# A running sum kept by sixteen accumulating transfers from GpSimd's queue in place of fifteen additions, with the program's order written anew

## The chip, the core and the metric

The kernel runs on one core of a Trainium2 chip. The metric is the device time of one execution in microseconds (us), lower is better. The core's engines are TensorE (PE in the profile; PEld is its weight load), VectorE (DVE), ScalarE (ACT) and GpSimd (POOL); SyncE (SP) issues nearly all transfers. Each engine works through its own instructions in the order in which the program gives them, and an instruction that waits holds those behind it on its engine.

## What is computed

A transformer block over 2048 tokens of width 512: a linear attention with a learned feature map (32 heads of width 16), then a spatial-shift mixer with two gelu layers. The part that the change touches is the attention's denominator:

```python
phi_k = concat([softmax(pk), softmax(-pk)])      # 2048 tokens x 32 heads x 32
kv = einsum("bhsf,bhsd->bhfd", phi_k, v)
z  = einsum("bhsf->bhf", phi_k)                  # the sum of phi over the tokens
num = einsum("bhqf,bhfd->bhqd", phi_q, kv)
den = einsum("bhqf,bhf->bhq", phi_q, z)[..., None] + 1e-6
o = (num / den) @ wo
```

## The kernel before

The tokens lie in 16 tiles of 128 rows, two of them to a chunk of 256. The program has these stages, and one stage's end overlaps the next one's beginning:

- Up to about 23 us: the modulation vectors, the first weights, the first layer norm.
- About 23 to 150 us: for each chunk the layer norm, its transposes (`pt`) and split `hh`; then projections of the keys, values and queries. A key tile goes from PSUM (`pp`) through `softmax_in` (two reductions `k1` and a subtraction on VectorE into `ke`, the exponentials on ScalarE), a sum and a reciprocal `k2` on VectorE, and the product `ke <- ke, k2`, which is now phi of that tile, mostly on GpSimd. `kv_add` then lets PE add the tile's 32x64 products into `kva`, and adds the tile into `zacc` (`za` in the profile), 128 partitions x 1024 values, 512 KB. Query tiles go through the same softmax (`qt`, `q1`, `qe`) and are stored to `q_s` in device memory.
- At the end of that stage two products with a matrix of ones sum `za` over the partitions and spread it (`zbc`, one of the tiles called `const`).
- About 153 to 330 us, chunk by chunk (`phase_a`): the query tiles come back (`e`), `ez <- e, const` is their product with `zbc`, VectorE makes the denominators (`pz`, `q2`, `q3`, `q5`), `e <- e, q3` divides, VectorE turns the tile into `pT`, and PE multiplies `pT` with `kvb` (the numerators); then `oT`, the output projection, two layer norms (`n`, `h`), and the mixer's first layer (`nT`, `pa`). `split_w3` (`wr`, `ws`) prepares weights in between, and `load_w` makes the halves `w` of each weight (`w <- raw, w` is the subtraction that gives the low half).
- From about 325 us on: the channel mixer with its weights streamed from device memory (`wq`), its partial sums in `pa` and `ac`; PE alone sets the pace there.

All work is first recorded as operations of a `Plan`, numbered in the order of recording. The table `ORDER` then lists all 2800 of them in the order in which they are emitted; a letter behind a number (A, V, G) chooses another engine for it than the first (ScalarE, VectorE, GpSimd). The table `SLOT` says which buffer each tile takes, so two tiles in one buffer wait for each other. Both tables come from a planner outside the kernel, which uses the costs written in the calls of `plan.op` (the engine's time, and `land`, the time until a transfer has landed). Waits between engines are set from the tiles that an operation reads and writes.

Of the kernel before, what the change touches and what calls it, by code (L numbers as in the profile page):

```python
# [11 lines left out]
OP = mybir.AluOpType  # L12
# [153 lines left out]
)  # L166
SLOT = {
    "pp": "051437620517022653373705745013034226461611710656607547246172461505207616274027341060462123674114"
          "3625706350706774303670237",
    "bd": "ag",  # L170
    "w": "0423679a50486cd35b7089",
    "rk": "k53e1blf",
# [1207 lines left out]
```

## Time and profile before

| | |
|---|---|
| median of three runs | 572.0 us (570.32 to 572.49) |
| the profiled execution | 576.09 us, span from first to last instruction 574.2 us |
| mean granted TensorE clock | 0.991 |
| PE busy | 558.8 us (97% of the span) |
| DVE, ACT, POOL busy | 497.1, 337.7, 377.1 us |
| share of the 16 DMA engines | 64.1% of the span for the queue that SP issues to |

The profiled execution lies 4.1 us above the median, and 1.9 us of it lie outside its span. PE is the engine that sets the pace over nearly the whole span; what is left of it is spread over single places. Times of rows below are counted from the span's start; "idle before" is the time that an engine stood still ahead of a group.

### The profile page before, as it was taken

How to read it: one execution, taken by the hardware profiler on the slowest of the kernel's cores; microseconds unless marked ns; L12 is line 12 of the kernel's file. 1: busy time of each engine (PE TensorE's matmuls, PEld its weight loads, DVE VectorE, ACT ScalarE, POOL GpSimd, SP SyncE). 2: the span in 40 equal slices, each digit the busy share in tenths (PEclk: the TensorE clock that was granted, in tenths of full speed). 3: DMA queues.
4: the chain of work that ended last, by engine and by line, in shares of the span. 5: the costliest groups of instructions: out<-in, count | busy, mean ns of one | idle time of the engine just before them, and what ended most of it. 6: DMA issues, size and time to landing. Idle time of an engine off the chain costs nothing.

```text
span 574.2 us, 12213 instructions
## 1 busy us (share of the span) xinstructions
PE 558.8 (97%) x4460; PEld 505.6 (88%) x4460; DVE 497.1 (87%) x899; ACT 337.7 (59%) x802; POOL 377.1 (66%) x390
## 2 busy tenths in 40 slices
PE   9999999999999699999999999999999999999996
PEld 9988878878788478888779999988999999999996
DVE  3789999999989999999997779858789868987987
ACT  2889896623423678697678866675652443544440
POOL 2579899997689999999774746435442535322532
PEclk9799999999999999999999999998999999999999
DMA  9964640631487656767569999994797696647222
GB/s 330 316 209 148 194 155 20 220 90 56 142 293 248 206 171 192 274 209 230 185 222 330 297 303 324 327 312 131 282 297 275 237 319 230 184 139 302 74 74 74
DMA packets 56251, 123.79 MB, mean 216 GB/s; under 512 B 6304, under 2 KB 17824, under 8 KB 52096
## 3 DMA queue, kind: packets, MB, share of 16 engines
q1 hardware_dynamic: 55904, 122.95, 64.1%
q8 instruction: 35, 0.57, 0.4%
q14 instruction: 24, 0.20, 0.1%
q10 hardware_dynamic: 288, 0.07, 0.1%
HBM read 88.66 MB, written 34.34 MB: 214 GB/s over the span
## 4 chain that ended last, share of the span: by engine, by line
PE 54%; DVE 4%; DMA 4%; POOL 4%; issue 1%; ACT 1%; DVEq 0%; POOLq 0%; SPq 0%
PE pa L472 23%; PE ac L472 18%; PE pp L472 12%; DMA xb<-dram 2%; DMA dram<-yt 2%; POOL ez L421 1%; PE pt L481 1%; POOL e L421 1%; POOL ws L421 1%; DVE pp L438 1%; DVE tw L419 0%; POOL w L421 0%; DVE q L443 0%; DVE pz L443 0%; POOL rs L582 0%
## 5 line engine op out<-in xcount | busy, mean ns | idle before, releaser
L472 PE MATMUL pa<-bH,wq 128*128 128x256 f32 x840 | 108.1, 283 | 2.6 <-DVE cu L419 2.6
L472 PEld LDWEIGHTS pa<-bH,wq 128*128 128x128 f32 x840 | 104.0, 190 | 3.5 <-DVE cu L419 2.8
L472 PE MATMUL ac<-w,gg 128*128 128x256 f32 x840 | 106.6, 281 | 0.0
L472 PEld LDWEIGHTS ac<-w,gg 128*128 128x128 f32 x840 | 103.2, 188 | 0.9
L472 PE MATMUL pp<-w,hh 128*128 128x512 f32 x384 | 94.5, 398 | 0.0
L472 PEld LDWEIGHTS pp<-w,hh 128*128 128x128 f32 x384 | 70.5, 188 | 16.0 <-issue 0.5
L472 PE MATMUL pp<-w,sh 128*128 128x512 f32 x192 | 49.2, 399 | 0.0
L472 PEld LDWEIGHTS pa<-nT,w 128*128 128x128 f32 x384 | 46.4, 189 | 2.8 <-DVE nT L419 1.7
L472 PE MATMUL pp<-w,oT 128*128 128x512 f32 x192 | 47.4, 397 | 1.4 <-DVE oT L419 1.4
L472 PE MATMUL pa<-nT,w 128*128 128x256 f32 x384 | 47.6, 283 | 1.0 <-DVE nT L419 1.0
L472 PE MATMUL pp<-hh,w 128*128 128x256 f32 x384 | 48.0, 282 | 0.0
L472 PEld LDWEIGHTS pp<-hh,w 128*128 128x128 f32 x384 | 46.2, 188 | 2.0 <-issue 0.9
L421 POOL TENSOR_TENSOR gg<-cu,gg 128x256 fp32r<-128x256 f32 (+1 forms) x33 | 22.5, 692 | 33.9 <-PE ac L472 12.4
L472 PEld LDWEIGHTS pp<-w,oT 128*128 128x128 f32 x192 | 35.4, 188 | 9.9 <-DVE oT L419 2.0
L472 PEld LDWEIGHTS pp<-w,sh 128*128 128x128 f32 x192 | 34.7, 188 | 8.9 <-issue 1.6
L402 ACT ACTIVATE cu<-pa 128x512 f32<-128x512 f32 (+1 forms) x39 | 20.4, 529 | 37.5 <-PE pa L472 29.2
L421 POOL TENSOR_TENSOR ez<-e,const 128x1024 f32<-128x1024 f32 x14 | 34.3, 2456 | 4.9 <-ACT const L402 3.5
L582 POOL TENSOR_TENSOR rs<-mv,const 128x2 f32<-128x2 f32 x31 | 21.9, 707 | 18.2 <-ACT mv L589 16.1
L421 POOL TENSOR_TENSOR e<-e,q 128x1024 f32<-128x1024 f32 x15 | 30.2, 2026 | 2.1 <-DVE q L419 2.1
L402 ACT ACTIVATE qe<-qe 128x512 f32<-128x512 f32 x32 | 19.3, 626 | 20.6 <-POOL qe L421 17.5
L402 ACT ACTIVATE gg<-sg 128x512 fp32r<-128x512 f32 x35 | 21.6, 623 | 15.2 <-DVE sg L419 11.0
L421 POOL TENSOR_TENSOR ke<-ke,k 128x1024 f32<-128x1024 f32 x15 | 29.1, 1946 | 0.6 <-DVE k L446 0.6
(219 smaller groups left out, 1294.4 us busy)
## 6 DMA issues: line engine op xcount, KB each, us to landing
wq<-dram SPq DMA_DIRECT2D x32, 1024.0 KB, 6.8
dram<-ws SPq DMA_DIRECT2D x35, 256.0 KB, 3.1
xl<-in_x SPq DMA_DIRECT2D x32, 256.0 KB, 4.1
dram<-qe SPq DMA_DIRECT2D x16, 512.0 KB, 2.9
e<-dram SPq DMA_DIRECT2D x16, 512.0 KB, 4.2
raw<-in_w SPq DMA_DIRECT2D x18, 256.0 KB, 4.3
mod<-in_wmod SPq DMA_DIRECT2D x16, 256.0 KB, 4.3
dram<-xl SPq DMA_DIRECT2D x16, 256.0 KB, 3.4
```

Source lines behind the costliest of these rows:

```text
L402: nc.scalar.activation(o(), i(), func, **kw)
L421: pool = ("Pool", cost, lambda: nc.gpsimd.tensor_tensor(o(), a(), b(), op=op))
L438: nc.vector.scalar_tensor_tensor(o(), a(), get(s), b(), op0=op0, op1=op1, **kw)
L472: nc.tensor.matmul(o(), a(), b(), start=s, stop=e, **kw)
L481: nc.tensor.transpose(o(), i(), ident())
L582: plan.op("Pool", 540 + 10 * m, lambda: nc.gpsimd.tensor_tensor(r(), v(), mhalf[:, :m](), op=OP.pow), [r], [v, mhalf])
```

## The change

`kv_add` no longer adds. The first tile's phi is copied into `zacc` by a transfer issued from GpSimd's queue, and each of the other fifteen is added to it by a transfer that reads the tile, adds it to what stands in `zacc` and writes that back. That makes 16 transfers where there were 15 additions (the first addition took two tiles). Each of them reads and writes all of `zacc`, so it waits on GpSimd's queue until the one before has landed. The planner counted 1 us of GpSimd and 3 us until landing for each, and with other rates for transfers wrote both tables anew: nearly every line of `ORDER` and `SLOT` differs.

```diff
@@ ORDER, SLOT: all lines anew, the first of each
-    "0 3 247 12 45 6 249 38 156 2 52 58 26 55 11 1 248 39 13 46 14 8 47 48 40 49 41 158 157 61 7 42 5 43 44V 19G "
+    "13 3 157 6 45 2 5 159 158 38 26 55 52 58 8 0 34 61 321 4 30 21 89G 46 19G 20G 47 91 48 39 49 101 92G 50 11 9 "
-    "za": "7",
+    "za": "1",
@@ kv_add
         first.append(e)
         if tt_:
-            tt(zacc, first[0] if tt_ == 1 else zacc, e, OP.add, "any")
+            plan.op("Pool", 1000, lambda: nc.gpsimd.dma_start(zacc(), e(), accum_op=OP.add), [zacc], [zacc, e], land=3000)
+        else:
+            plan.op("Pool", 1000, lambda: nc.gpsimd.dma_start(zacc(), e()), [zacc], [e], land=3000)
```

What the new order looks like at three places (names carry the numbers of their buffers, which differ between the two programs).

First, GpSimd's queue in the middle of the key stage. Before, `za` additions stand among the products `ke <- ke, k2` and the parts of w3 (`ws`):

```order
L421 TENSOR_TENSOR za_190_846<-za_190_846,ke_224_1021 128x1024
L421 TENSOR_TENSOR ke_230_1056<-ke_230_1056,k2_251_1215 128x1024
L421 TENSOR_TENSOR za_190_846<-za_190_846,ke_230_1056 128x1024
L421 TENSOR_TENSOR ke_253_1219<-ke_253_1219,k2_275_1331 128x1024
L421 TENSOR_TENSOR ws_256_1225<-ws_256_1225 128x256
L421 TENSOR_TENSOR za_190_846<-za_190_846,ke_253_1219 128x1024
```

Now, counted from 0, these are transfers 3 (`ke_191`), 4 (`ke_213`) and 5 (`ke_198`), with what stands between them:

```order
L421 TENSOR_TENSOR ke_191_859<-ke_191_859,k2_228_1055 128x1024
L789 DMA za_210_947<-ke_191_859 128x1024
L421 TENSOR_TENSOR ws_242_1130<-ws_242_1130 128x256
L421 TENSOR_TENSOR ke_219_1017<-ke_219_1017,k2_251_1178 128x1024
L421 TENSOR_TENSOR ws_229_1061<-wr_120_510,ws_229_1061 128x256
L789 DMA za_210_947<-ke_213_953 128x1024
L421 TENSOR_TENSOR ke_198_880<-ke_198_880,k2_214_961 128x1024
L421 TENSOR_TENSOR ke_250_1176<-ke_250_1176,k2_261_1282 128x1024
L789 DMA za_210_947<-ke_198_880 128x1024
```

The tiles are no longer added in the order in which they become phi, and two or three other instructions stand between one transfer and the next.

Second, VectorE ahead of the reciprocal `k2_228`, on which transfer 3 rests (`pp_238` is the key projection of a later tile, `hh_247` a half of the chunk after it). In the new order it reads:

```order
L443 TENSOR_REDUCE k1_245_1148<-pp_238_1103 128x32
L411 TENSOR_SCALAR pt_230_1064<-pt_230_1064,const_65_259 128x256
L443 TENSOR_REDUCE k1_245_1148<-pp_238_1103 128x32
L446 RECIPROCAL k2_226_1036<-k2_226_1036 128x64
L419 TENSOR_TENSOR hh_247_1155<-pt_230_1064,hh_247_1155 128x512
L419 TENSOR_TENSOR ke_250_1176<-pp_238_1103,k1_245_1148 128x1024
L443 TENSOR_REDUCE k2_251_1178<-ke_219_1017 128x64
L446 RECIPROCAL k2_228_1055<-k2_228_1055 128x64
```

In the order before, the same stretch of VectorE's instructions holds two of the four additions that it did:

```order
L419 TENSOR_TENSOR za_190_846<-za_190_846,ke_183_810 128x1024
L419 TENSOR_TENSOR za_190_846<-za_190_846,ke_197_873 128x1024
L443 TENSOR_REDUCE k1_235_1118<-pp_233_1082 128x32 x2
L419 TENSOR_TENSOR hh_223_1016<-pt_206_908,hh_223_1016 128x512
L443 TENSOR_REDUCE k2_242_1147<-ke_224_1021 128x64
```

The additions are gone, and the reciprocal stands behind reductions of `pp_238` that have nothing to do with it.

Third, GpSimd from the last of the sum to the first product with `zbc`. Before:

```order
L421 TENSOR_TENSOR za_190_846<-za_190_846,ke_298_1505 128x1024
L421 TENSOR_TENSOR ke_319_1676<-ke_319_1676,k2_327_1768 128x1024
L421 TENSOR_TENSOR ke_311_1613<-ke_311_1613,k2_320_1678 128x1024
L421 TENSOR_TENSOR za_190_846<-za_190_846,ke_311_1613 128x1024
L421 TENSOR_TENSOR ws_237_1133<-ws_237_1133 128x256
L421 TENSOR_TENSOR ez_351_1954<-e_273_1324,const_347_1898 128x1024
```

Now transfers 13, 14 and 15, and behind them:

```order
L789 DMA za_210_947<-ke_298_1529 128x1024
L421 TENSOR_TENSOR ke_315_1677<-ke_315_1677,k2_325_1741 128x1024
L789 DMA za_210_947<-ke_315_1677 128x1024
L421 TENSOR_TENSOR ws_197_875<-ws_197_875 128x256
L789 DMA za_210_947<-ke_323_1712 128x1024
L411 TENSOR_SCALAR mod_240_1118<-mod_240_1118,const_45_186 128x512
L421 TENSOR_TENSOR w_346_1934<-raw_260_1279,w_322_1706 128x512
L421 TENSOR_TENSOR acc_293_1493<-acc_293_1493,mod_240_1118 128x512
L421 TENSOR_TENSOR ws_286_1439<-ws_286_1439 128x256
L421 TENSOR_TENSOR w_346_1934<-raw_331_1771,w_322_1706 128x512
L421 TENSOR_TENSOR ez_358_2026<-e_336_1815,const_354_1955 128x1024
```

Low halves of weights (`w <- raw, w`) that stood behind the first `ez` before stand ahead of it now. The products with ones stand a little later on PE: the matmuls ahead of them are the same but for 24 more of a query projection (`pp <- hh, w`, 128x256) and one more tile's 16 into `kva`.

More of the change, by code (lines that the diff above doesn't have):

```diff
@@ L40 @@
 ORDER = (
[125 rows of a table removed]
[125 rows of a table added]
 )
 SLOT = {
[L168 to L172, printed above, removed]
-    "xl": "3148067ekjf2b3k5lj53ea310b4kb36f9ej72ka7ja8ci0f3",
-    "st": "12701i7g069dej37c25di54f801d1e691",
-    "mv": "53bd32a2f80g169dej3ej87277g6ci84a",
-    "rs": "64eg45dji4af280g169fh9a5dbi3fhbde",
-    "nm": "89afch89j6bch5e137bcih54abfih84g2630cj40acehb9agj25370cf",
@@ L178 @@
-    "xn": "9h7d2i38lg461g7j",
-    "acc": "efj90c",
-    "mod2": "0213",
-    "kva": "3",
-    "za": "7",
-    "hh": "158bcd1e",
-    "pt": "34142601145004722001432070140451",
-    "raw": "c9j016dcegb32dj7fh6fich05376",
-    "k1": "2040342352052250",
-    "ke": "6480536481534086",
-    "k2": "3150104314340143",
-    "vv": "8ai2de3a2728lg8e",
-    "qe": "5792013575963459",
-    "q1": "1352115204253304",
-    "qt": "44b66g8g0c6k",
-    "mod": "5084351a2ihb3fhl",
-    "kvs": "6",
-    "pz": "5",
-    "q2": "03125452",
@@ L197 @@
-    "e": "9214026381032509",
-    "ez": "4548788095254818",
-    "q3": "1245043013013041",
-    "q5": "11215024",
-    "pT": "8681859658808758",
-    "oT": "bcece2e1",
-    "nT": "b1bcee11",
-    "n": "08j2j2ea6jhe5005",
-    "h": "g68l75c2a84legi9",
-    "gf": "25133058",
-    "sh": "271b2be0",
-    "pa": "230137237075120265423717201420003710223716262317332611112637",
-    "wr": "12776",
-    "ws": "546kld8ihlf8229d04k24h31g0aj1h33bg9",
-    "gb": "d",
-    "tw": "42241",
-    "bL": "19619160",
@@ L214 @@
-    "nb": "g19i1bbf641f9g1i",
-    "yt": "04jc2k8a4k84lkk3",
-    "bH": "37852370594053597856709424173812",
-    "tr": "1kjb59g9hehflf02",
-    "wq": "7a92ae1942e142a14e2142ea14aa241ae124",
-    "cu": "2lhb6acjfk05b4l29cfi56e3ab9jf08ecf7hi06g",
-    "gl": "e70k0k1i",
-    "ac": "73565436014546500146475061205431",
-    "gg": "82430784237689470624708634560438294352687102543987153894567039456827013298576140",
-    "sg": "g541542ehgjke1haj1i474g2lfc6g5a5415l69ek",
-    "xb": "8k387gh841b9j3c4",
-    "uu": "lf8c2aa1l9b6",
@@ L226 @@
-    "xc": "17e6b0517ialg825",
+    "pp": "310025647016523417562234574731201310560527164404207515162200742145522637756435042453503473755764"
+          "6456232662403100407456656",
+    "bd": "9a",
+    "w": "023467abe809d7c2aeb589",
+    "rk": "d586j1be",
+    "xl": "4103lik5146e0b4cgcl0b45djgk930i12bf8dc0l063f23f6",
+    "st": "410di20bg58gf16bdj5gh57d8922gf346",
+    "mv": "629f167fi4be258gf16f1be15b3ce2cj7",
+    "rs": "83bg39d1297ij40e238i6gf34a86a15bf",
+    "nm": "a57cehj548aec3hj60adhc397aihc40dj49aih097ec0jb7dih809gea",
@@ new lines @@
+    "xn": "kg2fcgi2981kd8eg",
+    "acc": "h33hld",
+    "mod2": "1023",
+    "kva": "3",
+    "za": "1",
+    "hh": "1589cd15",
+    "pt": "34027056465646277632207075053017",
+    "raw": "46cdjaf55ef193gf61ieah9ij8a2",
+    "k1": "0152312122504213",
+    "ke": "4503872450892765",
+    "k2": "4503450133255404",
+    "vv": "fgj5932b3bc1fi5e",
+    "qe": "7821333921596134",
+    "q1": "2304402153452213",
+    "qt": "920e81i8j958",
+    "mod": "j8hbf07d9d37cigj",
+    "kvs": "9",
+    "pz": "1",
+    "q2": "10451314",
@@ new lines @@
+    "e": "8047802905693258",
+    "ez": "3639217883206107",
+    "q3": "2352130240520532",
+    "q5": "00405143",
+    "pT": "3215738231100623",
+    "oT": "34575144",
+    "nT": "363775b1",
+    "n": "j1gj7fi91ibhf8kf",
+    "h": "23l80c75lj6g5b71",
+    "gf": "73591127",
+    "sh": "146514b8",
+    "pa": "472302073015637342706313405452116040257345626763442053310242",
+    "wr": "69674",
+    "ws": "8282d40fkc7796i7eh9e113df2hf02aefib",
+    "gb": "4",
+    "tw": "70813",
+    "bL": "94590138",
@@ new lines @@
+    "nb": "3g2k32ek2c961i9a",
+    "yt": "k637fchgh2j83ck3",
+    "bH": "65207869847158519793554369622730",
+    "tr": "cfeki370dh9ih2i2",
+    "wq": "365314630413604314630463106160413604",
+    "cu": "ld0e5bghk7d2ga7eicf39ghbdf0l36a1gh0ije3k",
+    "gl": "7jk1j538",
+    "ac": "26376173541052105367765316703524",
+    "gg": "02137261030426103476249583652347832769017985642107410371549685421785036297184503",
+    "sg": "ifklkic680h6859b83687i5c21987c7d68f6ad7g",
+    "xb": "1l0l52eak6lb9c1l",
+    "uu": "khfii72ab7jd",
@@ L227 @@
+    "xc": "9fjf0ag3j32256fk",
 }
```

248 rows, old and new, of the table ORDER are left out of this document.

## The prediction

> **What bounds the kernel now.** I read the page's busy line first, then who PE waited for, then busy time by stretch.
>
> ```profile
> PE 558.8 (97%) x4460; PEld 505.6 (88%) x4460; DVE 497.1 (87%) x899; ACT 337.7 (59%) x802; POOL 377.1 (66%) x390
> ```
> ```profile
> PE pp L472 <- DVE pT L758: 3.3, 3, 1.6
> PE pa L472 <- DVE cu L419: 2.6, 1, 2.6
> PE pp L472 <- DVE oT L419: 1.4, 1, 1.4
> PE pa L472 <- DVE nT L419: 1.0, 1, 1.0
> ...
> PE pp L472 <- DVE const L419: 0.5, 1, 0.5
> PE pt L481 <- ACT n L402: 0.5, 1, 0.5
> ```
> ```profile
> 80.00:100.00 20.00, 20.00 (x164) 16.40 (x164) 18.84 (x26) 13.39 (x30) 18.27 (x17) 1.00 0.12 38
> 100.00:125.00 25.00, 25.00 (x231) 20.26 (x230) 23.88 (x33) 12.68 (x24) 24.84 (x16) 1.00 0.54 167
> 125.00:150.00 25.00, 25.00 (x263) 21.52 (x263) 24.54 (x32) 9.46 (x17) 19.66 (x11) 1.00 0.21 66
> 150.00:175.00 25.00, 24.47 (x318) 20.89 (x317) 22.87 (x33) 8.54 (x19) 20.06 (x11) 1.00 0.78 262
> 175.00:200.00 25.00, 20.63 (x148) 16.54 (x146) 23.59 (x43) 13.39 (x33) 25.00 (x18) 1.00 0.64 210
> 200.00:225.00 25.00, 24.11 (x209) 20.09 (x210) 24.23 (x40) 20.44 (x47) 25.00 (x21) 1.00 0.56 179
> 550.00:574.00 24.00, 19.30 (x152) 18.57 (x151) 19.10 (x43) 3.99 (x12) 6.89 (x8) 1.00 0.20 67
> ```
>
> The waits are in us in total, times, longest; the stretches give stretch, length, busy PE, PEld, DVE, ACT, POOL, clock, DMA share, GB/s. PE is busy in all of 80 to 150 us, where the additions lie: faster engines there save nothing by themselves. What can be saved lies behind: 3.3 + 1.4 + 0.5 + 0.5 = 5.7 us between 170 and 205, while DVE and POOL are full; 1.0 (nT) and 2.6 (cu) later; some 4.7 at the end, where the last additions follow the last matmul. All PE work stays: the new order has the same 20 kinds of matmul in the same numbers. So the change can give some 9 us at most, and lose without limit if PE comes to wait.
>
> **What goes.** The additions:
>
> ```profile
> L421 POOL TENSOR_TENSOR za<-za,ke x10: 2390/2408/2436, 78.9 to 146.6; 128x1024 f32<-128x1024 f32 x10
> L419 DVE TENSOR_TENSOR za<-za,ke x4: 1210/1218/1656, 81.5 to 145.2; 128x1024 f32<-128x1024 f32 x4
> ...
> L472 PE MATMUL pp<-za,const x4: 591/592/592, 150.0 to 151.3; 128*128 128x512 f32 x4
> L421 POOL TENSOR_TENSOR za<-ke,ke x1: 2433/2433/2433, 64.6 to 64.6; 128x1024 f32<-128x1024 f32 x1
> ```
>
> 10 x 2.41 + 2.43 = 26.5 us of POOL and some 5.3 us of DVE are freed, all under a full PE: nothing by themselves.
>
> **Where PE now asks for the sum.** Before, at 149.97:
>
> ```profile
> 149.97 1.88 PE L472 MATMUL pp<-za,const 128*128 128x512 f32 x4
> 151.78 0.65 PE L472 MATMUL kva<-ke,vv 128*32 128x64 f32 x32
> 152.36 3.09 PE L472 MATMUL pp<-hh,w 128*128 128x256 f32 x24
> ```
>
> The matmuls ahead of it in the new order are one query projection (24, 3.0 us net) and one tile's kva (32 records, 0.6) more, so a PE that never waits asks at 149.97 + 3.6 = 153.5.
>
> **When the sum is there.** Each transfer waits for the landing of the one before. I call L the time from the end of one transfer's wait to its landing; no row shows one. First the place from which the chain runs tight. Transfer 3 needs the product of ke_191, and that the reciprocal k2_228, which VectorE has behind reductions of pp_238. Ahead of pp_238's end PE has 180 matmuls of 512 columns and 96 of 256, as many as ahead of the end of this row, with four transposes more and 16 kva fewer, which cancel:
>
> ```profile
> 84.50 3.05 PE L472 MATMUL pp<-w,hh 128*128 128x512 f32 x12
> ```
>
> That is 87.5. Durations of what follows:
>
> ```profile
> L443 DVE TENSOR_REDUCE k<-pp 128x32 f32<-128x512 f32 x32 | 20.5, 667 | 0.4 <-PE pp L472 0.3
> L419 DVE TENSOR_TENSOR ke<-pp,k 128x1024 f32<-128x1024 f32 x16 | 19.3, 1205 | 0.2
> L443 DVE TENSOR_REDUCE k<-ke 128x64 f32<-128x1024 f32 x16 | 19.2, 1200 | 1.2 <-ACT ke L402 0.6 <-issue 0.3
> L419 DVE TENSOR_TENSOR hh<-pt,hh 128x512 fp32r<-128x512 f32 x16 | 10.8, 679 | 0.3 <-ACT hh L402 0.2
> L446 DVE RECIPROCAL k<-k 128x64 f32<-128x64 f32 x16 | 8.6, 540 | 0.1
> L411 DVE TENSOR_SCALAR pt<-pt,const 128x256 f32<-128x256 f32 x12 | 6.4, 545 | 2.0 <-PE pt L481 1.9
> L421 POOL TENSOR_TENSOR ke<-ke,k 128x1024 f32<-128x1024 f32 x15 | 29.1, 1946 | 0.6 <-DVE k L446 0.6
> L421 POOL TENSOR_TENSOR w<-raw,w 128x512 fp32r<-128x512 f32 x13 | 17.1, 1312 | 4.0 <-ACT w L402 3.6 <-PE pp L472 0.3
> ```
>
> On VectorE 2 x 0.67 + 0.55 + 2 x 0.54 + 0.68 + 1.21 + 1.20 = 6.0, less some 0.2 since neighbours overlap: 93.3. Then POOL's product, 1.95: transfer 3 goes at 95.3. From there POOL has never more than about 4.2 us of other work between two transfers (ke_254's product and three parts of ws of 0.75 ahead of transfer 7), so for L from 4.4 up the landings alone set the pace: twelve links to transfer 15 and its own landing, 95.3 + 13 L. (Transfer 0 could go at about 73 by the same count, so transfers 0 to 2 bind only from L = 7.4.) PE waits X = 95.3 + 13 L - 153.5; the chain is in time up to L = 4.48, and each 0.1 us of L costs 1.3 us of PE. That is the term on which this forecast rests.
>
> **L from rows.** Transfers of known size (KB each, median us from issue to landing, then the one of 1 MB that starts between 250 and 300):
>
> ```profile
> dram<-qe SPq DMA_DIRECT2D x16, 512.0 KB, 2.9
> e<-dram SPq DMA_DIRECT2D x16, 512.0 KB, 4.2
> out_dram<-xb SPq DMA_DIRECT2D x4, 128.0 KB, 1.8
> wq<-dram SPq DMA_DIRECT2D x32, 1024.0 KB, 6.8
> ```
> ```profile
> wq<-dram SPq DMA_DIRECT2D x1, 1024.0 KB, 5.4
> ```
>
> Lower end: 2.9, as if the second read and the making of the transfer by GpSimd were free. Upper end: 6.8, as much data as is read here, on full DMA engines. Between: from 128 to 512 KB a store grows by 1.1 us, so 512 KB more by 1.5, which gives 4.4; the least crowded row of 1 MB says 5.4. GpSimd has still to make the transfer, for which I add the upper half of that gap: L = 5.0. It is nearest to the 1 MB row, since each transfer reads the tile and zacc, 2 x 512 KB, and the DMA engines are half busy or less there (0.54, 0.21). The Trainium skill, "DMA: Bandwidth & Descriptors", Anatomy of one DMA — SWDGE (gpsimd) path, puts a transfer from GpSimd at 2.0 us plus its bytes at 436 GB/s, an estimate of 3.2 us for 512 KB, by which the chain would be in time; no row before shows such a transfer. The Trainium skill, "Collectives: The Full Stack", The bandwidth ceiling, speaks against taking that figure: an add in the DMA engine reads two sources, and its rate was measured at about half a copy's; 2.0 + 2.4 = 4.4 would be that estimate, still just in time.
>
> **The sum.** With L = 5.0 the last landing is at 160.3 and X = 6.8 us. Behind it, POOL goes from the sum to the third chunk's numerators. Before:
>
> ```profile
> 153.16 5.32 POOL L421 TENSOR_TENSOR ez<-e,const 128x1024 f32<-128x1024 f32 x2 [3.46 <-ACT const L402]
> ```
> ```profile
> 204.75 0.67 PE L472 MATMUL pp<-pT,const 64*32 64x256 f32 x16 [0.56 <-DVE pT L758]
> ```
>
> Between the two POOL is nearly full. In the new order three subtractions w<-raw,w (1.31 each) and one smaller piece of w (0.9) of that stretch stand ahead of the first ez: 4.8 us less. The sum is asked for 3.6 later, so without X the numerators of that chunk come 1.2 us earlier, and of the 5.7 us that PE waits there some 4.5 stay. X adds in full: while PE stands at the products with ones, neither zbc nor ez can go on. The subtractions moved forward cost nothing; POOL does them while transfer 15 is under way (X also covers them). Other moves I take at nothing: from 215 to 569 us PE shows only 3.6 us of waits to win. The load of the transfers, 16 x 1 MB read and 0.5 MB written over some 85 us, falls where the DMA share is 0.12 to 0.54 and I cost it at nothing on SP's loads, which are issued well ahead.
>
> Behind the waiting transfers stand products that kva needs; the nearest is ke_198, behind transfer 4 (100.3 + 1 + 2 = 103.3), which PE wants at about 104; if it slips, PE waits there instead and the last wait shrinks by as much. Buffers of ke are held until landing; VectorE wants the one of transfer 8 (lands at 125.3) at about 135.
>
> Against the profiled execution: 576.09 + 6.8 - 1.2 = 581.7; against the median, 4.1 lower, 577.6 us.
>
> **Rivals.**
> 1. The chain is in time: L up to 4.5 (the interpolated stores, 4.4). X = 0: 572.0 - 1.2 = 570.8, no change that can be told (I take 0.5%, 2.9 us, as what a measurement of this kernel can tell). With L to 4.8 X is up to 4.1 and it still is none. Against it: it needs the transfer to be made by GpSimd at no cost.
> 2. Faster: in time, and the new order also takes away the waits for cu (2.6) and nT (1.0): 570.8 - 3.6 = 567.2. Its place is PE at 272 and 388; it decides if VectorE, with 5.3 us less behind it, has those two adds done before PE arrives. For it: both waits are on DVE. Against: the same number of other instructions was laid anew around them.
> 3. The transfer is much dearer, L = 5.8 to 6.8 (the crowded 1 MB row): X = 17 to 30, 588 to 601 us. For it: sixteen rows of DMA work in one queue with SP's; against: the load is light between 80 and 150.
> 4. The engine that makes the transfers holds the products: with over 2 us of POOL for each, POOL instead of landing paces the chain. It has the same end as L raised, 580 to 590, and is counted in 3 and in the forecast.
>
> **How the numbers follow.** The forecast (L 4.8 to 5.8, 575 to 588) has 0.45, rival 1 0.27, rival 2 0.16, rival 3 0.12. Slower: forecast and rival 3, less the share that other moves give back, 0.56; same 0.27; faster 0.17. The range leaves out most of rival 3 and the far end of rival 2: 567 to 589.
>
> **What would show it.** A row of POOL transfers za<-ke some 5 us apart from about 95 us on; the last landing near 160; PE idle some 7 us before pp<-za,const, with a transfer as releaser; POOL waiting between 95 and 160; waits of PE for pT of about 4 to 5 us as before. If the transfers land in 4.4 us or less, PE runs through at 153 and I am wrong; so also if reciprocals ahead of transfer 3 come earlier than counted.

## The result, and the profile after

| | before | changed |
|---|---|---|
| median of the runs side by side | 572.25 us (4 runs) | 592.29 us (4 runs) |
| ratio, 95% interval | 1 | 1.033 (1.029 to 1.037) |
| profiled execution, span | 576.09, 574.2 | 592.05, 590.3 |
| busy PE / DVE / POOL | 558.8 / 497.1 / 377.1 | 563.9 / 491.8 / 353.3 |

Slower by 20 us against a forecast of 5.6, and above the range of 567 to 589. The two profiled executions are only 16.1 us of span apart, because the one before had come out 4 us above its median; the accounts below go from one to the other.

Page of the changed kernel, busy line, and behind it whom TensorE waited for (us in total, times, longest):

```profile
PE 563.9 (96%) x4460; PEld 508.9 (86%) x4460; DVE 491.8 (83%) x904; ACT 339.2 (57%) x807; POOL 353.3 (60%) x381
```
```profile
PE pp L472 <- DMA za<-ke: 10.5, 1, 10.5
PE kva L472 <- DVE vv L411: 5.3, 1, 5.3
PE pp L472 <- DVE pT L758: 1.9, 1, 1.9
PE pp L472 <- DVE qe L419: 1.6, 1, 1.6
```

New waits: 10.5 + 5.3 + 1.6 = 17.4. Matmuls of the same number are 563.9 - 558.8 = 5.1 longer. Gone: all 2.6 for cu, 1.4 for oT, 0.5 + 0.5, and 1.4 of the 3.3 for pT; some 6.5 with smaller ones. 17.4 + 5.1 - 6.5 = 16.0 of the 16.1 us. Part of the 6.5 may belong to that one execution of the kernel before and not to the change: in the run of the old order with transfers (below) the wait for cu is 0.6 and not 2.6.

The timeline of TensorE (start, us, work, idle before it and what ended that) shows the two waits and the slow stretch behind each:

```profile
141.88 2.91 PE L472 MATMUL pp<-w,hh 128*128 128x512 f32 x12
150.08 1.94 PE L472 MATMUL kva<-ke,vv 128*32 128x64 f32 x64 [5.29 <-DVE vv L411]
151.94 4.32 PE L472 MATMUL pp<-w,hh 128*128 128x512 f32 x12
...
157.22 5.92 PE L472 MATMUL pp<-hh,w 128*128 128x256 f32 x48
173.68 3.78 PE L472 MATMUL pp<-za,const 128*128 128x512 f32 x4 [10.54 <-DMA za<-ke]
```

Twelve matmuls that take 2.91 us before the first wait take 4.32 behind it, and the four products with ones take 3.78 where they took 1.88. With the `kva` rows behind the two waits (1.94 and 1.66 for 64 that take 1.10 elsewhere) that is 2.25 us behind the first wait and 2.46 behind the second, 4.7 of the 5.1 us. (A third slow stretch, behind the 1.9 us wait for pT, has its like in the kernel before, behind the wait for cu.) TensorE asks for the sum at 157.22 + 5.92 = 163.1, not at 153.5, and gets it at 173.7.

GpSimd's timeline gives the transfers. Rows 4, 9, 10, 14, 15 and 16 of the sixteen:

```profile
94.86 0.90 POOL L789 DMA_DIRECT2D za<-ke  x1 [0.30 <-POOL ke L421]
...
123.01 0.88 POOL L789 DMA_DIRECT2D za<-ke  x1 [1.52 <-DMA za<-ke]
...
132.39 0.88 POOL L789 DMA_DIRECT2D za<-ke  x1 [5.27 <-DMA za<-ke]
133.00 4.13 POOL L421 TENSOR_TENSOR ke<-ke,k 128x1024 f32<-128x1024 f32 x2
...
153.67 0.87 POOL L789 DMA_DIRECT2D za<-ke  x1 [1.13 <-DMA za<-ke]
...
161.50 0.88 POOL L789 DMA_DIRECT2D za<-ke  x1 [4.98 <-DMA za<-ke]
...
169.11 0.89 POOL L789 DMA_DIRECT2D za<-ke  x1 [5.96 <-DMA za<-ke]
```

Transfer 3 goes at 94.86, as forecast (95.3). Transfer 15 goes at 169.11, twelve links later (a link is the time from the start of one transfer to the start of the next): 6.19 us each. By the times from issue to landing each of them starts 0.2 to 0.7 us behind the landing before it. The links are uneven: 9.38 from 123.01 to 132.39, 7.83 from 153.67, 7.61 from 161.50, and 4.9 to 6.0 for the other nine. The twelve take 14.25 us more than 12 x 5.0, and the three long ones make 9.8 of that. What three of them shared the DMA engines with stands in the views of the DMA work over these stretches (q0: GpSimd's transfers, q1: SyncE's loads and stores; packets, MB, share of 16 engines; then the transfer's time from issue to landing). First 132.39 to 137.5, where q1 carried nothing, then 153.67 to 161.5, then the longest, 123.01 to 132.39:

```profile
q0 software_dynamic: 144, 0.52, 54.2%
za<-ke POOLq DMA_DIRECT2D x1, 512.0 KB, 4.6
```
```profile
q1 hardware_dynamic: 509, 1.46, 55.5%
q0 software_dynamic: 144, 0.52, 39.2%
za<-ke POOLq DMA_DIRECT2D x1, 512.0 KB, 7.1
```
```profile
q1 hardware_dynamic: 816, 0.98, 37.6%
za<-ke POOLq DMA_DIRECT2D x1, 512.0 KB, 8.8
```

Alone a transfer lands 4.6 us behind its issue, beside 1.46 MB of other traffic 7.1, beside 0.98 MB 8.8. The third long link shared with 1.07 MB (7.0 us to landing), the other nine with 0.9 MB or less. The rate of that traffic does not put the links in order, though: the longest had less of it per us than four links of 5.5 to 6.0 us, in whose stretches the DMA share was 0.84 to 1.00, against 0.67 here. Why it took 9.38 us stays open.

The wait for `vv` comes from one of these links too. While GpSimd stands 5.27 us before transfer 9 (the row of 132.39), the products in its queue behind it stand as well (133.00). VectorE's timeline:

```profile
135.28 1.22 DVE L443 TENSOR_REDUCE k<-ke 128x64 f32<-128x1024 f32 x1 [5.44 <-POOL ke L421]
...
149.30 0.63 DVE L411 TENSOR_SCALAR vv<-pp 128x512 f32<-128x512 f32 x1
```

VectorE idles 5.44 us for such a product, and TensorE stands 5.29 us until `vv`, fourteen us further down VectorE's queue.

### The profile page after: what moved, and what is told of

Its sections match the earlier page's. It is cut to its first block, busy times and chain, and to the rows that moved or that the text cites. A ratio compares the mean times of both kernels' runs of the same rounds, so it can differ in the third digit from the quotient of the medians.

```text
span 590.3 us, 12230 instructions
## 1 busy us (share of the span) xinstructions
PE 563.9 (96%) x4460; PEld 508.9 (86%) x4460; DVE 491.8 (83%) x904; ACT 339.2 (57%) x807; POOL 353.3 (60%) x381
## 4 chain that ended last, share of the span: by engine, by line
PE 43%; DVE 7%; DMA 2%; issue 1%; ACT 0%; POOL 0%; SPq 0%; DVEq 0%; ACTq 0%
PE pa L472 20%; PE ac L472 18%; PE pp L472 4%; DMA dram<-h 1%; DVE pz L443 1%; DVE pp L438 1%; DMA xl<-dram 1%; DVE bH L419 0%; DVE xb L419 0%; DVE q L443 0%; DVE ez L419 0%; DVE nT L419 0%; DVE uu L419 0%; DVE oT L419 0%; DVE gg L419 0%
## 5 line engine op out<-in xcount | busy, mean ns | idle before, releaser
L472 PE MATMUL pa<-bH,wq 128*128 128x256 f32 x840 | 106.9, 281 | 0.0
L472 PEld LDWEIGHTS pp<-w,hh 128*128 128x128 f32 x384 | 71.8, 190 | 16.5 <-issue 0.2
L472 PE MATMUL pp<-hh,w 128*128 128x256 f32 x384 | 49.8, 288 | 1.6 <-DVE qe L419 1.6
L472 PEld LDWEIGHTS pp<-hh,w 128*128 128x128 f32 x384 | 48.1, 194 | 3.7 <-issue 2.8
L582 POOL TENSOR_TENSOR rs<-mv,const 128x2 f32<-128x2 f32 x31 | 24.5, 797 | 17.4 <-ACT mv L589 17.4
L789 POOL DMA_DIRECT2D za<-ke x15 | 13.2, 880 | 29.8 <-DMA za<-ke 23.7
L402 ACT ACTIVATE gg<-cu 128x256 fp32r<-128x256 f32 (+1 forms) x57 | 19.0, 356 | 19.9 <-PE ac L472 16.4
L419 DVE TENSOR_TENSOR cu<-pa,cu 128x512 f32<-128x512 f32 (+1 forms) x36 | 21.2, 597 | 10.3 <-PE pa L472 7.1
```

Of the source, the lines that this page charges most:

```text
L402: nc.scalar.activation(o(), i(), func, **kw)
L419: dve = ("DVE", 71 + 1.04 * o.n + 90 * (isps(a) and isps(b)), lambda: nc.vector.tensor_tensor(o(), a(), b(), op=op))
L472: nc.tensor.matmul(o(), a(), b(), start=s, stop=e, **kw)
L582: plan.op("Pool", 540 + 10 * m, lambda: nc.gpsimd.tensor_tensor(r(), v(), mhalf[:, :m](), op=OP.pow), [r], [v, mhalf])
L789: plan.op("Pool", 1000, lambda: nc.gpsimd.dma_start(zacc(), e(), accum_op=OP.add), [zacc], [zacc, e], land=3000)
```

## The experiments

Two theories. **T**: the transfers lose the time, since GpSimd's queue waits for each landing. **R**: the new order starves TensorE whoever adds.

**Additions in the new order** (each fourth on VectorE; the first tile is copied by an instruction of GpSimd):

```diff
-plan.op("Pool", 1000, lambda: nc.gpsimd.dma_start(zacc(), e(), accum_op=OP.add), ...)
+eng = nc.vector if tt_ % 4 == 3 else nc.gpsimd
+plan.op("Pool", 2332, lambda: eng.tensor_tensor(zacc(), zacc(), e(), op=OP.add), ...)
```

> The new order and buffers, with the sixteen transfers turned back into one copy and fifteen additions at the same places (three of four on GpSimd, each fourth on VectorE). Theory T (the loss comes from the transfers: their landings hold up GpSimd's queue, and what stands behind it starves the matmuls): the waits for vv (5.3 us), qe (1.6) and for the sum (10.5) and the 5.1 us of slower matmuls go, the 6.5 us of waits recovered later stay: 565 to 574 us. Rival R (the new order itself starves the matmuls, whoever adds): 585 us or more, with a wait of 4 us or more between 140 and 175 us.

579.11 us against 572.76 of the kernel before, run beside it; ratio 1.010 (1.008 to 1.013). Between the two forecasts: the wait for the sum is gone, but the one for `vv` stands:

```profile
PE kva L472 <- DVE vv L411: 4.1, 1, 4.1
```

By this run 13 of the 20 us go with the transfers, and I had to ask whether VectorE's four additions (one took 2.95 us at 137.87) or the order made the rest.

**All additions on GpSimd:** as above with `eng = nc.gpsimd` throughout.

> The new order with the copy and all fifteen additions on GpSimd (15 x 2.4 us), none on VectorE. If the 4.1 us wait for vv in the new order with additions came from the four additions that VectorE had there, it goes, and GpSimd's last addition comes 3 to 8 us after the products with ones are asked for: 573 to 580 us. If it is the order itself, the wait for vv stays at 4 us: 578 to 584 us.

582.37 us against 574.64; ratio 1.013 (1.009 to 1.017). The two forecasts overlap and the kernel before ran 2 us slower beside it, so the total does not decide between them; the wait for `vv` does, which stays, at 5.6 us, so it was not made by VectorE's four additions. The stretches (length; busy PE, PEld, DVE, ACT, POOL; clock, DMA share, GB/s) suggest why:

```profile
100.00:125.00 25.00, 23.66 (x192) 20.03 (x191) 17.77 (x24) 13.29 (x27) 24.84 (x17) 1.00 0.41 138
125.00:150.00 25.00, 22.72 (x169) 18.51 (x167) 24.30 (x30) 7.64 (x15) 24.84 (x15) 1.00 0.25 82
```

GpSimd is busy 24.84 of 25 us twice over; in the kernel before it was 24.84 and 19.66. The new order has filled the room that the additions left there, and with them back TensorE waits for GpSimd's products (2.3 us) as well as for `vv`. So far R holds: with additions in it this order starves TensorE.

**Transfers in the old order** (the first addition stays):

```diff
-            tt(zacc, first[0] if tt_ == 1 else zacc, e, OP.add, "any")
+            if tt_ == 1:
+                tt(zacc, first[0], e, OP.add, "any")
+            else:
+                plan.op("Pool", 1000, lambda: nc.gpsimd.dma_start(zacc(), e(), accum_op=OP.add), ...)
```

> The order and buffers of the kernel before, with its first addition kept and the other fourteen turned into accumulating transfers at the same places of the order, all on GpSimd's queue. T: the chain of landings is late at the products with ones here too, and the products behind it in GpSimd's queue are late: 580 to 600 us. R: the transfers cost little by themselves: 570 to 576 us.

601.68 us against 572.76; ratio 1.050 (1.046 to 1.053), as T has it and a little above its range:

```profile
PE pp L472 <- DMA za<-ke: 20.4, 1, 20.4
```

The chain loses in both orders. The old order's own loads are enough to lengthen it: the last eleven transfers, from 106.84 on, take 4.5 to 8.4 us from issue to landing, 5.7 on average, where the changed kernel's thirteen from transfer 3 on take 5.6. The two slowest (7.1 and 8.4) lie beside 1.2 and 1.6 MB of other traffic, the four fastest (4.5 to 4.7) beside 0.5 MB or less.

**Two accumulators**, tiles in turn, everything else as in the changed kernel:

```diff
-    zacc = T("za", [P, 2 * D])
+    zacc = [T("za", [P, 2 * D]), T("const", [P, 2 * D])]
...
+        za = zacc[tt_ % 2]
...
-        mms([(..., ones, zacc[:, j * D:(j + 1) * D], True, True)], ...)
+        mms([(..., ones, zacc[i][:, j * D:(j + 1) * D], i == 0, i == 1) for i in range(2)], ...)
```

> The changed kernel with two accumulators that take the transfers in turn, so that each transfer waits for the landing of the one but last; the products with ones add both up (four more records of 0.59 us, 2.4 us of TensorE). T: no wait of GpSimd for a landing over 2 us, no wait of TensorE over 2 us near 145 and 165: 566 to 576 us. R: as the changed kernel plus 2.4 us: 590 to 596 us. If a transfer's landing is as late as it is because the DMA engines are full rather than because the chain waits, two in flight land later each, and some 4 to 8 us of the waits stay: 577 to 585 us.

The first tile of each accumulator is copied, so there are two copies and fourteen accumulating transfers. Some small constants share a buffer to make room for the second accumulator.

577.10 us against 572.76; ratio 1.007 (1.004 to 1.010), and 15 us under the changed kernel though TensorE has 2.4 us more to do. The profile shows no wait of GpSimd for the landing of a transfer any more, and of TensorE's new waits there are left:

```profile
PE pp L472 <- DMA const<-ke: 2.5, 1, 2.5
PE pp L472 <- DMA za<-ke: 1.0, 1, 1.0
```

That settles T against R for the bulk: the order is the same, and but for the one more copy so are the transfers; each now waits for the landing of the one but last instead of the last. It does not come out quite as T had it: 577.10 lies 1.1 above T's range and at the lower end of the third case, whose reason (4 to 8 us of waits left, since the DMA engines are full) is not far off: TensorE still waits 3.5 us for the last landings.

**Plain copies**; the sum is left out, the waits stay:

```diff
-nc.gpsimd.dma_start(zacc(), e(), accum_op=OP.add)
+nc.gpsimd.dma_start(zacc(), e())
```

> The changed kernel with plain copies in place of the accumulating transfers, each still waiting for the one before; the sum is left out (the last tile stays). If the second read of an accumulating transfer costs what its bytes do (Theory B), the link falls by some 1.2 us (half of the 2.4 us that the packets of the last transfer flow) and the wait for the sum is gone: 570 to 580 us. If the link is the making, the descriptors and the landing (Theory F), it stays at 4.5 us and more: 588 to 594 us.

576.78 us against 572.76; ratio 1.005 (1.002 to 1.008). The total is Theory B's, and so is the link: 61.0 us for the twelve from transfer 3 to 15, 5.09 each, 1.1 less than with the add (GpSimd waits 6.4 us for landings where it waited 23.7). But of the wait for the sum, which was to go, half is left.

```profile
PE pp L472 <- DMA za<-ke: 5.3, 1, 5.3
```

The wait for `vv` is gone. So what the add puts on top of a copy, over the length of the chain, makes most of the loss: 15.5 of the 20 us.

**The links by themselves:**

```diff
+    for i in range(6):
+        send(za, ke[i % 2])           # accumulate, alone
...
+    loads(30, 6)                      # SyncE: 512 KB each, six in flight
+    for i in range(6):
+        send(za, ke[i % 2])
...
```

> No layer is computed: stages of six 512 KB transfers from GpSimd's queue, each waiting for the landing before, (1) accumulating and alone, (2) plain copies and alone, (3) accumulating beside loads of 512 KB with six in flight, (4) beside loads with one in flight, (5) accumulating 256 KB and alone, (6) two chains in turn alone, (7) two chains beside six loads, (8) one chain beside back-to-back additions of VectorE. Theory C (the link is some 4.5 us by itself and grows with what else the DMA engines carry): start to start 4.5 to 5 us in (1), 3.3 in (2), 8 us or more in (3), 5 to 7 in (4), 3.2 to 3.8 in (5), 4.5 to 5 for a pair in (6). Rival S (the link grows with the work of GpSimd and VectorE, which share their way to memory): (3) and (4) as (1), and (8) 6 us or more.

GpSimd's timeline; the second and third transfer of the stages alone, copy, beside six loads, beside one load, 256 KB, two chains, beside VectorE:

```profile
23.55 0.87 POOL L371 DMA_DIRECT2D const<-const  x1 [3.98 <-DMA const<-const]
28.35 0.86 POOL L371 DMA_DIRECT2D const<-const  x1 [3.94 <-DMA const<-const]
...
53.51 0.54 POOL L373 DMA_DIRECT2D const<-const  x1 [2.61 <-DMA const<-const]
56.70 0.53 POOL L373 DMA_DIRECT2D const<-const  x1 [2.65 <-DMA const<-const]
...
82.70 0.87 POOL L371 DMA_DIRECT2D const<-const  x1 [9.75 <-DMA const<-const]
91.51 0.86 POOL L371 DMA_DIRECT2D const<-const  x1 [7.94 <-DMA const<-const]
...
134.94 0.86 POOL L371 DMA_DIRECT2D const<-const  x1 [4.75 <-DMA const<-const]
140.75 0.86 POOL L371 DMA_DIRECT2D const<-const  x1 [4.95 <-DMA const<-const]
...
180.19 0.88 POOL L371 DMA_DIRECT2D const<-const  x1 [2.77 <-DMA const<-const]
183.84 0.87 POOL L371 DMA_DIRECT2D const<-const  x1 [2.77 <-DMA const<-const]
...
211.59 0.86 POOL L371 DMA_DIRECT2D const<-const  x1 [2.00 <-DMA const<-const]
214.59 0.86 POOL L371 DMA_DIRECT2D const<-const  x1 [2.13 <-DMA const<-const]
...
317.06 0.88 POOL L371 DMA_DIRECT2D const<-const  x1 [4.04 <-DMA const<-const]
322.09 0.87 POOL L371 DMA_DIRECT2D const<-const  x1 [4.15 <-DMA const<-const]
```

Start to start: 4.80 alone, 3.19 for a copy, 8.81 beside six loads, 5.81 (5.6 to 6.8 over that stage) beside one, 3.65 for half the bytes, 3.00 with two chains (2.6 to 3.0 over that stage), 5.03 beside VectorE's additions. In the seventh stage, two chains beside six loads, a transfer takes 3.8 to 5.0, some 4.4 on average, half of one chain's 8.81. Theory C holds in every stage but the sixth, which I had put at 4.5 to 5 for a pair: two transfers in turn take 5.4 to 5.9 once both are under way. S is out: VectorE's work adds some 0.2 us at most. If the time is a straight line in the bytes, which two sizes cannot show, a link is some 2.5 us that do not go with the bytes (3.65 - 1.15) and 1.15 per 256 KB; the add takes 1.6 of the 4.80. And one load in flight on SyncE's queue gives links of the size that the changed kernel has on average (6.19).

**A wait and the clock:** bursts of 160 matmuls with growing waits between.

> No layer is computed: eight bursts of 160 matmuls (128x512, fp32r) on TensorE, and between them waits for GpSimd that grow from about 1 to about 13 us. Theory K (in the changed kernel TensorE's clock halves for some 4.6 us after its waits of 5.3 and 10.5 us, which makes the 5.1 us by which its matmuls are longer; waits of 1.6 us leave it alone): from some wait between 2 and 5 us on, the first some 4.5 us of the next burst are at 0.50, whatever the length of the wait, so that each long wait costs some 2.3 us more than itself. Rival: the slower stretch grows with the wait, or the clock falls for another reason and all bursts run alike.

Timeline, and the first 10 us of the second, third and eighth burst (length, busy PE, clock, DMA share, GB/s):

```profile
45.23 36.58 PE L345 MATMUL pz<-const,const 128*128 128x512 f32 x160 [0.92 <-POOL const L372]
84.06 38.16 PE L345 MATMUL pz<-const,const 128*128 128x512 f32 x160 [2.25 <-POOL const L372]
...
304.34 39.33 PE L345 MATMUL pz<-const,const 128*128 128x512 f32 x160 [10.65 <-POOL const L372]
```
```profile
45.23:55.23 10.00, 10.00 (x44) 1.00 0.01 2
84.06:94.06 10.00, 10.00 (x37) 0.83 0.01 2
304.34:314.34 10.00, 10.00 (x32) 0.70 0.00 0
...
84.06:85.06 1.00, 1.00 (x4) 0.96 0.00 0
85.06:88.06 3.00, 3.00 (x8) 0.50 0.03 5
...
301.34:302.34 1.00, 0.00 (x0) 0.50 0.00 0
```

A burst behind a wait of 2.25 to 10.65 us is 1.5 to 2.8 us longer than the one behind 0.92, with no clear growth between. K holds in the main: the price of a wait is around its 2.3 us. The moment of the fall is not where K had it. Behind 2.25 us TensorE had stopped at 45.23 + 36.58 = 81.81, and the clock fell 1 us after the burst had begun again (the fourth and fifth row); a mean of 0.96 over 84.06 to 85.06 puts the fall at 84.98, 3.2 us after the stop. In the longest wait it is down before the burst begins (the last row). Read in the same way, the fall comes 2.7 to 3.8 us after the stop in the four waits of 2.25 to 4.74 us.

In the kernels there is no sharp threshold. Waits of 1.94 us (changed kernel, at 211.55), 2.16 (plain copies), 2.21 (old order with transfers) and 2.59 (kernel before, for cu) were followed by a clock of 0.50; waits of 2.12 (two accumulators), 2.27 (the late adds below) and 2.70 (old order with transfers, at 110.38) were not. All waits of 4 us and more were, and none of 1.41 to 1.62. The changed kernel's two new long waits at 1.5 to 2.8 us each make 3.0 to 5.6, which covers its 5.1 us.

**Two chains, late tiles added:** tiles 0 to 12 go to two accumulators in turn; GpSimd adds tiles 13 to 15 and the two accumulators.

```diff
+        za = zacc[tt_ % 2 if tt_ < 14 else 0]
+        if tt_ > 12:
+            def add():
+                nc.gpsimd.tensor_tensor(za(), za(), e(), op=OP.add)
+                if tt_ == NT - 1:
+                    nc.gpsimd.tensor_tensor(za(), za(), zacc[1](), op=OP.add)
```

> The changed kernel with two accumulators for tiles 0 to 12 in turn; tiles 13 to 15 are added by GpSimd, and so are the two accumulators at the end (2.4 us each), so TensorE's products with ones stay four records. If the landings at the end are all that is left against the order (3.5 us of waits and 2.4 us of records in the kernel with two accumulators, 577.1 us), it comes to 570 to 573 us, level with the kernel before or a little under. If the transfers slow the rest by contention, 574 to 578.

574.07 us against 574.64 (12 and 17 runs); ratio 1.000 (0.998 to 1.002). By its time alone that is the case of contention (574 to 578). But the forecasts took some 572 us for the kernel before, which ran 574.64 beside this one, and to be level with it is what the first case says. TensorE runs through to 147.63 + 5.92 = 153.55 and waits 0.86 there:

```profile
147.63 5.92 PE L472 MATMUL pp<-hh,w 128*128 128x256 f32 x48
154.41 1.98 PE L472 MATMUL pp<-za,const 128*128 128x512 f32 x4 [0.86 <-POOL za L794]
```

All of the loss is taken back, and no more: the best version found is level with the kernel before. So the new order by itself, with a GpSimd free of most of the sum, costs nothing that can be told, and R is out for the changed kernel.

## Why the prediction was wrong

- **What goes: right in the main.** 5.3 us of VectorE's work went, and 23.8 of GpSimd's where 26.5 were forecast. That it buys nothing by itself fits the version with late additions, which is level with the kernel before.
- **Where TensorE asks: right if it isn't starved.** 153.5 forecast; 153.55 in the version with late additions, 163.1 in the changed kernel, after 6.9 us of waits and the slow clock.
- **Where the chain starts: right**, 94.86 for 95.3 (the reciprocal ahead of transfer 3 ended at 92.53 for 93.3), and landings pace it from there.
- **The transfer by itself: right**, with some luck, since no row before showed such a transfer. L = 5.0 forecast, 4.8 measured alone. The estimate of 3.2 us after the Trainium skill, "DMA: Bandwidth & Descriptors", Anatomy of one DMA, is that of the plain copy (3.19). The other estimate, 4.4 us, which halves the rate for the add after the Trainium skill, "Collectives: The Full Stack", The bandwidth ceiling, was near for the accumulating one (4.80).
- **The step that failed: L as one number, 5.0 for all thirteen landings**, taken for DMA engines that "are half busy or less there (0.54, 0.21)". "The load of the transfers ... I cost it at nothing" asks what the transfers do to SyncE's loads and never what those loads do to the transfers. In the changed kernel the same stretches, the transfers included, read (the DMA share is the last number but one):

```profile
100.00:125.00 25.00, 25.00 (x243) 20.42 (x242) 20.58 (x30) 15.37 (x31) 19.61 (x19) 1.00 0.86 226
125.00:150.00 25.00, 18.17 (x90) 14.67 (x88) 19.49 (x25) 7.27 (x14) 13.47 (x11) 0.96 0.68 157
```

Shares of 0.86 and 0.68. The link became 6.19, and the last landing came at 94.86 + 12 x 6.19 + 4.5 = 173.6, where 160.3 was forecast. That makes X = 173.6 - 153.5 = 20.1 us in place of 6.8: 14.3 us from twelve links that were each 1.2 us longer than forecast, less 1.0 since the chain began 0.4 earlier and its last landing took 4.5. The new order's traffic was not needed for it; with transfers in the old order the landings took as long (5.7 us for 5.6).
- **"If it slips, PE waits there instead and the last wait shrinks by as much": right in the sum, wrong in the place.** I looked at the products that TensorE reads; what slipped was a product that VectorE reads, and through VectorE's queue `vv`, for 5.3 us. The 6.9 us of earlier waits and the 2.3 of slow matmuls behind them are part of the 20.1, since TensorE then asked later.
- **"X adds in full": too little.** Behind the last wait came 2.5 us of half-speed matmuls on top of X.
- **Given back: 6.5, not 1.2.** The wait for cu did vanish, as the second rival had it, and so did oT's. That rival's own condition, a chain in time, did not hold, so this part of the result is luck, and some of it may belong to the one profiled execution before. From the forecast of 5.6: + 13.3 for the chain, + 2.5 for the clock, - 5.3 given back, is 16.1, the distance of the two profiled executions.
- The third rival, "much dearer", had the size (588 to 601 for L of 5.8 to 6.8) and the reason (one row of work with SyncE's); I gave it 0.12, on the DMA shares of the old order. That its total came out so well is in part luck: it left out the clock and most of what was given back.

What stays open: that the loads made the three long links inside the kernel is read from their stretches, from the old order with transfers and from the stages beside loads; the amount of traffic beside a link does not by itself give its length, and a run of the whole kernel without those loads was not tried.

## What to carry to other kernels

A chain of transfers that each wait for the landing before is a serial engine of its own: take its link under the traffic that will run beside it, multiply by its length, and forecast a range as wide as that product, not as wide as one link. Break the chain (here two accumulators gave back 15 of 20 us) before asking whether the transfer is cheaper than the instruction. And a queue that waits for a transfer holds all that stands behind it: follow those rows to the engines that read them, one queue further than the first.

## What the runs showed of the hardware

- An accumulating 512 KB transfer inside on-chip memory takes 4.80 us, a copy of the same 3.19; two independent ones in turn 2.6 to 3.0 each (start to start, in the stages by themselves).
- Six loads in flight nearly double it (8.81), one in flight adds 0.8 to 2.0 us. Two chains in turn beside six loads take some 4.4 us per transfer.
- TensorE's clock fell to 0.50 behind every wait of 4 us or more, behind none of 1.62 us or less that was looked at, and behind some of 1.94 to 2.77 us but not all (2.12, 2.27 and 2.70 us left it at 1.00). In the bursts it fell 2.7 to 3.8 us after the last matmul, even where work had begun again by then (waits of 2.25 and 2.77 us), and a burst ran 3.2 to 5.9 us at 0.50. The Trainium skill, "TensorE: Matmul & The Clock Gate", Part 1, tells of idle gaps over some 3.4 us; here shorter ones were enough in most cases.
